# Sharing the early normalizations of an attention + PReLU-MLP kernel among three engines, with a new order of transfers and of attention pieces

## The chip, the cores and the metric

One core of one Trainium2 chip. The metric is the device time of one execution in microseconds (us). A time below is the median of a kernel's executions, which were all in the fast state except in runs 3 and 10, where the slow ones are named. The kernel before takes 353.95 us (353.81 to 354.05, four runs). Engine names in the profiles: PE is TensorE's matmuls, DVE is VectorE, ACT is ScalarE, POOL (Pool in the text) is GpSimd, SP is SyncE. PSUM is the memory into which the matmuls write, SBUF the general on-chip memory.

## The reference, cut to what matters

```python
# q, k, v: (8 batches, 8 heads, 576 positions, 64), float32
scores = q @ k.T / 8
# heads 0..3: local mask (0 <= i-j < 32); heads 4..7: strided mask (j <= i, j % 32 == i % 32)
attn = softmax(where(mask, scores, -1e9))
x = (attn @ v)  ->  (4608 tokens, 512)
h = x @ w_in                                 # 512 -> 2048
g = max(h, 0) + alpha * min(h, 0)
out = g @ w_out                              # 2048 -> 512, float32
```

The 4608 tokens are worked off in nine blocks of 512. Block 0 of layer 1 needs batch 0 of the attention, block 1 needs batch 1. Each batch has two units: the local heads and the strided heads, two pairs of heads in each.

## The kernel before

Attention is a list of small pieces that are emitted one by one between the matmuls of the two layers: T (transposes of q and k), S (scores and exponentials), P (attention times v, "PV", with the normalization), X (transpose back, into `xT`). A PV piece ends with a reciprocal of the row sums and a product, both on VectorE, read from PSUM:

```python
def pv_piece(P, a):
    ...                                      # up to 6 matmuls into pv (pool "ps", 3 PSUM buffers)
    keep(nc.vector.reciprocal(rc[0:w, 0:nb], pvv[:, :, 64]))
    keep(nc.vector.tensor_tensor(P.x16[...], pvv[:, :, 0:64], rc[...].to_broadcast(...), op=ALU.mult))
```

`keep` fixes the order: each engine executes its instructions in the order in which the program emits them. That includes the transfers: those issued by Pool (among them all that cast from float32 to float16) stand in Pool's instruction stream.

The pieces of the first two batches, and the start of the program:

```python
def alone(u0, u1):                           # u0 the strided unit, u1 the local one
    ...                                      # T(u0), S(u0) x4, T(u1), S(first pair of u1) x2,
    ...                                      # P(u0) x6, S(second pair of u1) x2, X(u0) x2, P(u1) x4, X(u1) x2

keep(nc.sync.dma_start(consts, consts_dram)) # SyncE: constants, q, k of the strided heads of batch 0
load_qk(0, True, "q")
load_qk(0, True, "k")
...                                          # Pool: rest of batch 0, w_in parts 0 to 2, strided q, k of
...                                          # batch 1, w_in part 3, v and local q, k, v of batch 1
for i in range(end0):                        # batch 0: pieces with filler matmuls between
    attn_step(end0); warm(4 if i < 2 else 1)

for c in range(4):
    load_w(c, True)                          # Pool: four w_out parts
cast_l(1, "q"); cast_l(1, "k"); ...          # Pool: casts of batch 1
load_unit(2, False); load_unit(2, True)      # Pool: ten transfers of batch 2
for m in range(16):                          # block 0 of layer 1
    lin1_piece(0, m, True)
    attn_n(0 if m < 9 else 1, end1)          # 7 pieces of batch 1 ride along
while pos["i"] < end1:
    attn_step(end1)                          # the other 19 pieces alone; then block 1
```

The softmax here doesn't subtract the row's maximum and nothing guards it: scores larger than these inputs give would overflow.

## Time and profile before

Start times from the records of the profiled run (span 352.0 us):

| | us |
|---|---|
| first k lands, cast on ScalarE begins | 7.59 |
| block 0 begins | 26.58 |
| local q, k of batch 1 transposed | 44.31, 44.76 |
| last transfer of batch 2 that Pool has to issue (stv, v of the strided heads) | 56.41 |
| block 1 begins | 57.06 |
| span | 352.0 |

Read it as two intervals: up to block 0 (26.6 us) and from block 0 to block 1 (30.5 us). After that TensorE is nearly always busy, and what is lost before it is not regained. The lines themselves stand in the prediction.

### The profile page before, as it was taken

What the parts mean: (1) busy time and instruction counts of PE and PEld (TensorE: products, weight loads), DVE (VectorE), ACT (ScalarE), POOL (GpSimd) and SP (SyncE); (2) the same over time, 40 slices, a digit from 0 to 9 for tenths busy, and PEclk for the clock granted to TensorE, in tenths of its full rate; (3) what the DMA queues carried; (4) which work ended last, traced back from release to release, by engine and by line L of the source; (5) the groups of instructions that cost most, each with busy time, mean ns of one, the idle gap of its engine ahead of it and who ended that gap; (6) DMA issues with size and microseconds to landing.
All of it is one profiled execution on the core that took longest, in us unless ns stands there. A gap on an engine that the chain in (4) does not pass through costs nothing.

```text
span 352.0 us, 6757 instructions
## 1 busy us (share of the span) xinstructions
PE 336.4 (96%) x2733; PEld 175.7 (50%) x2733; DVE 198.3 (56%) x391; ACT 176.6 (50%) x313; POOL 147.4 (42%) x164
## 2 busy tenths in 40 slices
PE   7899979999898998999999999999999999999995
PEld 2554544454444544554467665545455444444444
DVE  3487774884443875576557655765575444444400
ACT  2635852665336574656465646565645444444411
POOL 7936726259895583656365532451240000000000
PEclk9999985999999999999999999999999999999999
DMA  7999999934946862553556210000001100100021
GB/s 232 185 203 224 234 253 151 184 34 69 160 99 176 75 164 57 87 48 61 177 85 62 49 47 31 32 31 32 30 32 40 52 30 31 61 30 30 32 89 61
DMA packets 46111, 33.08 MB, mean 94 GB/s; under 512 B 27376, under 2 KB 37760, under 8 KB 46080
## 3 DMA queue, kind: packets, MB, share of 16 engines
q0 software_dynamic: 37312, 16.79, 44.6%
q1 hardware_dynamic: 8768, 15.87, 12.8%
q8 instruction: 21, 0.34, 0.4%
q14 instruction: 10, 0.08, 0.1%
HBM read 36.83 MB, written 9.44 MB: 131 GB/s over the span
## 4 chain that ended last, share of the span: by engine, by line
PE 86%; DVE 4%; POOL 4%; ACT 3%; DMA 1%; issue 1%; SPq 0%; ACTq 0%
PE hps L489 36%; PE ops L534 32%; PE sp L271 3%; PE tp L214 3%; PE pv L318 3%; DVE x L327 2%; PE xp L335 2%; POOL et L305 2%; DMA ql<-in_q_dram 1%; PE wps L556 1%; ACT kT L159 1%; PE sp L287 1%; PE ops L525 1%; ACT osb L539 1%; PE sph L287 1%
## 5 line engine op out<-in xcount | busy, mean ns | idle before, releaser
L502 DVE SCALAR_TENSOR_TENSOR gT<-neg,oma,hps 128x512 f16<-128x512 f32 x144 | 106.9, 743 | 74.7 <-ACT neg L499 72.4
L489 PE MATMUL hps<-xT,win 128*128 128x512 f16 (+1 forms) x640 | 146.7, 361 | 0.1
L534 PE MATMUL ops<-wout,gT 128*128 128x512 f16 x560 | 141.9, 379 | 1.9 <-ACT osb L539 1.6
L499 ACT ACTIVATE neg<-hps 128x512 f32<-128x512 f32 x144 | 86.2, 599 | 95.1 <-PE hps L489 93.6
L305 POOL TENSOR_TENSOR et<-et,consts 128x576 f16<-128x576 f16 (+1 forms) x48 | 61.3, 1277 | 80.5 <-ACT et L295 80.4
L489 PEld LDWEIGHTS <-win 128*128 128x128 f16 x640 | 58.4, 98 | 52.9 <-issue 3.4
L534 PEld LDWEIGHTS <-gT 128*128 128x128 f16 x560 | 49.7, 97 | 50.7 <-issue 2.5
L295 ACT ACTIVATE et<-sp 72x576 f16<-72x576 f32 (+1 forms) x58 | 37.6, 649 | 24.8 <-PE sp L271 11.7
L327 DVE TENSOR_TENSOR x<-pv,rc 72x384 f16<-72x384 f32 (+2 forms) x80 | 42.1, 527 | 2.7
L325 DVE RECIPROCAL rc<-pv 72x6 f32<-72x6 f32 (+2 forms) x80 | 14.9, 187 | 41.7 <-PE pv L318 41.4
L539 ACT COPY osb<-ops 128x512 f32<-128x512 f32 x35 | 20.6, 587 | 27.9 <-PE ops L534 27.9
L318 PEld LDWEIGHTS <-et 72*128 72x128 f16 (+1 forms) x448 | 23.2, 99 | 17.1 <-DVE x L327 1.8
L271 PEld LDWEIGHTS <-kT 64*128 64x128 f16 x448 | 10.9, 95 | 27.8 <-issue 17.7
L271 PE MATMUL sp<-qT,kT 64*128 64x72 f16 (+1 forms) x408 | 17.6, 201 | 3.5 <-ACT kT L159 3.2
L161 DVE COPY qT<-tp 128x1024 f16<-128x1024 f16 (+1 forms) x16 | 17.4, 1085 | 4.1 <-PE tp L214 4.1
L159 ACT COPY kT<-tp 128x1024 f16<-128x1024 f16 (+1 forms) x16 | 14.5, 909 | 6.7 <-PE tp L214 6.7
L556 PE MATMUL wps<-wrm 128*128 128x512 f16 x44 | 16.4, 448 | 1.2 <-DVE wrm L568 1.2
L318 PE MATMUL pv<-vs,et 72*128 72x65 f16 x256 | 15.4, 194 | 2.1 <-POOL et L305 0.8
L335 PEld LDWEIGHTS <-x 72*128 72x128 f16 (+1 forms) x224 | 12.4, 102 | 7.6 <-DVE x L327 2.4
L335 PE MATMUL xp<-consts,x 72*128 72x72 f16 (+1 forms) x224 | 14.7, 208 | 1.0 <-DVE x L327 0.8
L163 POOL COPY vs<-stv 72x1024 f16<-72x1024 f16 x14 | 14.5, 1061 | 0.0
L318 PE MATMUL pv<-vl,et 128*128 128x65 f16 x192 | 12.0, 200 | 1.2 <-DVE vl L161 1.1
(66 smaller groups left out, 189.6 us busy)
## 6 DMA issues: line engine op xcount, KB each, us to landing
out_dram<-osb SPq DMA_DIRECT2D x35, 256.0 KB, 2.0
ql<-in_q_dram SPq DMA_DIRECT2D x6, 512.0 KB, 5.2
kl<-in_k_dram SPq DMA_DIRECT2D x6, 512.0 KB, 5.9
stv<-in_v_dram POOLq DMA_DIRECT2D x8, 288.0 KB, 5.3
vl<-in_v_dram POOLq DMA_DIRECT2D x8, 288.0 KB, 8.3
win<-in_moe_w_in_dram POOLq DMA_DIRECT2D x4, 512.0 KB, 10.3
wout<-in_moe_w_out_dram POOLq DMA_DIRECT2D x4, 512.0 KB, 16.8
qs<-in_q_dram POOLq DMA_DIRECT2D x7, 256.0 KB, 4.6
```

What stands on the lines that cost most here:

```text
L271: keep(nc.tensor.matmul(sps[y][:, w * x : w * x + w], P.kT[hf, k0 : k0 + 128], P.qT[hf, w * t : w * t + w], start=(x == 0), stop=(x == len ...
L295: keep(nc.scalar.activation(ev.rearrange("r (y c) -> r y c", y=2), sp[0:r, :, 0:n], AF.Exp, scale=SCALE))
L305: keep(nc.gpsimd.tensor_tensor(ev, ev, m, op=ALU.mult))
L318: keep(nc.tensor.matmul(pv[:, 65 * x : 65 * x + 65], et[0:r, c : c + 128], v16[0:r, 2 * P.pr + hh, t, :] if P.strided else v16[:, 6 * (2 * ...
L327: keep(nc.vector.tensor_tensor(P.x16[0:w, c0 : c0 + 64 * nb].rearrange("r (c e) -> r c e", e=64), pvv[:, :, 0:64], rc[0:w, 0:nb].unsqueeze ...
L335: keep(nc.tensor.transpose(xp[:, P.w * t : P.w * t + P.w], P.x16[0 : P.w, 128 * t : 128 * t + 128], ident[0 : P.w, 0 : P.w]))
L489: keep(nc.tensor.matmul(hps[:, dst : dst + w], win16[:, kk, 128 * m : 128 * m + 128], xT[:, kk, src : src + w], start=(kk == 0 and x == 0) ...
L499: keep(nc.scalar.activation(neg, hps, AF.Relu, scale=-1.0))
L502: keep(nc.vector.scalar_tensor_tensor(gTs[n][:, m, :], neg, oma[:, m : m + 1], hps, op0=ALU.mult, op1=ALU.add))
L534: keep(nc.tensor.matmul(ops, gTs[n][:, kf, 128 * mt : 128 * mt + 128], wout16[:, kf, :], start=(kf == 0), stop=(kf == 15)))
L539: keep(nc.scalar.copy(osb, ops))
L556: keep(nc.tensor.matmul(wps, wrm[:, 0:128], wrm, start=True, stop=True))
```

## The change

The intent: VectorE's chain of reciprocals and products gates both early attention stages. Half of the products go to ScalarE (a copy from PSUM to SBUF) and Pool (the product, from SBUF), transfers are issued between Pool's products so that Pool is not blocked by a long train of them, and the strided heads of batch 1 begin inside block 0 after the fourth of its 16 tiles (index 3) instead of the tenth (index 9).

```diff
+        if P.b < NEARLY and (a == 0 or (P.strided and P.pr and a == 1)):
+            pvs = rpool.tile([128, 390], F32, tag="pvs", bufs=2, name="pvs")
+            keep(nc.scalar.copy(pvs[0:w, 0 : 65 * nb], pv[0:w, 0 : 65 * nb]))
+            pvv = pvs[0:w, 0 : 65 * nb].rearrange("r (c e) -> r c e", e=65)
+            keep(nc.gpsimd.tensor_tensor(xo, pvv[:, :, 0:64], rc[...].to_broadcast(...), op=ALU.mult))
+            return
 ...
-        feed(T(u1, "q"), -1)                       # alone(): old order cut
+        rest = [Pv(g, i) for g in A for i in range(3)]
+        if together:                               # batch 0: local transposes between the PVs
+            rest[3:3] = [T(u1, "q")]
+            rest[5:5] = [T(u1, "k")]
+        else:                                      # batch 1: PVs, transposes back, then the local unit
+            rest += [X(A[0]), X(A[1]), T(u1, "q"), T(u1, "k")]
 ...
-            hps = pspool.tile([128, 512], F32, tag="ps", name="hps3")
+            hps = popool.tile([128, 512], F32, tag="ops", name="hps3")
 ...
+    load_qk(0, True, "q")
     keep(nc.sync.dma_start(consts, consts_dram))
-    load_qk(0, True, "q")
     load_qk(0, True, "k")
 ...
+    after = {                                      # batch 0: transfers behind pieces 6, 11, 13, 23
+        6: (lambda: load_tail(1, True), lambda: load_w(2, False)),
+        11: (lambda: load_v(1, True),),
+        13: (lambda: load_w(3, False),),
+        23: (lambda: load_qk(1, False, "q"),),
+    }
 ...
+    after = {                                      # block 0: transfers and casts behind tiles 1 to 15
+        1: (lambda: load_qk(1, False, "k"),),
+        3: (lambda: load_tail(1, False), lambda: load_v(1, False)),
+        8: (lambda: load_w(0, True), lambda: cast_v(1, 0, "pool"), lambda: cast_v(1, 1, "pool"),
+            lambda: load_w(1, True)),
+        12: (lambda: load_w(2, True),),
+        14: (lambda: cast_l(1, "q"), lambda: load_w(3, True)),
+        15: (lambda: cast_l(1, "k"),),
+    }
+    for m in range(16):
+        lin1_piece(0, m, True)
+        attn_n(0 if m < 3 else 1, end1)
+        for fn in after.get(m, ()):
+            fn()
     load_unit(2, False)
     load_unit(2, True)
-    for m in range(16):
-        lin1_piece(0, m, True)
-        attn_n(0 if m < 9 else 1, end1)
     wide["on"] = True
     while pos["i"] < end1:
         attn_step(end1)
```

## The prediction

> **What bounds the kernel now.** I read the page's 40 slices first, then the chain of waits up to 96 us in order of time, Pool's timeline, the stretches around the dip of the clock, and the groups by form.
>
> ```profile
> PE   7899979999898998999999999999999999999995
> POOL 7936726259895583656365532451240000000000
> PEclk9999985999999999999999999999999999999999
> DMA  7999999934946862553556210000001100100021
> ```
>
> A slice is 8.8 us. After slice 16 TensorE is full and the edit doesn't touch it. The edit works in slices 1 to 6: attention of batch 0 (with idle-filling matmuls), layer-1 block 0, attention of batch 1, start of block 1. DMA is full from slice 1 to 7, and in slices 5 and 6 the clock dips.
>
> ```profile
> 23.54 0.55 DVE x L327
> 24.09 0.11 DVE rc L325
> 24.21 0.02 issue
> 24.23 0.55 DVE x L327
> ...
> 26.56 0.47 DVE xT L343
> 27.03 0.04 issue
> 27.07 8.58 PE hps L489 x39
> ...
> 56.70 0.42 PE xp L335 x3
> 57.12 0.53 PE hps L489
> ```
>
> This is the chain. Runs of reciprocal plus product on VectorE (0.66 us a pair) gate both attention stages. Block 0 starts at 26.6 us (fully from 27.07), block 1 at 57.06. From the last score piece inside block 0 (43.45) to 57.06 only attention runs. Whatever moves the start of block 1 moves the end one for one, since what follows is unchanged.
>
> ```profile
> 50.00:51.00 1.00, 0.81 (x17) 0.50 (x14) 0.96 (x4) 0.00 (x0) 0.00 (x0) 0.85 1.52 302
> 51.00:52.00 1.00, 1.00 (x9) 0.34 (x8) 0.93 (x4) 0.45 (x1) 0.34 (x1) 0.50 1.76 270
> ...
> 60.00:61.00 1.00, 1.00 (x4) 0.30 (x3) 0.58 (x1) 0.09 (x1) 1.00 (x2) 0.53 1.20 205
> 61.00:62.00 1.00, 1.00 (x6) 0.48 (x5) 0.46 (x1) 0.61 (x2) 1.00 (x2) 1.00 1.09 255
> ```
>
> The granted clock (third number from the end) is 0.50 from 50.9 to 60.9 us, so block 1 runs 3.9 us at half speed and loses about 1.9.
>
> ```profile
> 47.23 0.72 POOL L111 DMA_DIRECT2D qs<-in_q_dram  x1 [4.17 <-DMA wout<-in_moe_w_out_dram]
> 49.11 0.71 POOL L111 DMA_DIRECT2D ks<-in_k_dram  x1 [1.16 <-DMA wout<-in_moe_w_out_dram]
> 51.66 0.57 POOL L130 DMA_DIRECT2D tl<-in_q_dram  x1 [1.85 <-DMA wout<-in_moe_w_out_dram]
> 53.66 0.55 POOL L130 DMA_DIRECT2D tl<-in_k_dram  x1 [1.42 <-DMA ql<-in_q_dram]
> 56.41 0.76 POOL L144 DMA_DIRECT2D stv<-in_v_dram  x1 [2.21 <-DMA kl<-in_k_dram]
> ```
>
> This is the view I weigh most. Counted in Pool's own order, every transfer waits for the one eight before it to land: the 32nd (qs of batch 2) for the 24th (second w_out part), the 36th (stv of batch 2) for the 28th (kl of batch 2), which lands at 56.1. The same holds at 16.57, 18.26, 21.68 and 24.32. In the kernel before nobody needs Pool between 38 and 57 us, so these waits are free.
>
> **What the Trainium skill says.** "GPSIMD Engine Reference", section 1: Pool has no PSUM access; hence the ScalarE copy ahead of each Pool product. Its section 3.1: about 2.6 cycles per element for a two-input operation at 1.2 GHz. For 576 columns that is 1,248 ns; the trace's mask products take 1,277, so it agrees. "DMA: Bandwidth & Descriptors", "Anatomy of one DMA": a wait for a semaphore is served by the issuing sequencer, not by the DMA engines. The lines above agree: Pool itself stands still. "TensorE: Matmul & The Clock Gate", Part 1: the clock halves after a sparse window of some 3.4 us and comes back after a busy one. The dip of 10.0 us (three windows) agrees.
>
> **The change part by part.**
>
> ```profile
> L327 DVE TENSOR_TENSOR x<-pv,rc 96x384 f16<-96x384 f32 x32 | 17.7, 553 | 1.1
> ...
> L305 POOL TENSOR_TENSOR et<-et,consts 128x576 f16<-128x576 f16 x24 | 30.7, 1278 | 48.1 <-ACT et L295 48.1
> ...
> L539 ACT COPY osb<-ops 128x512 f32<-128x512 f32 x35 | 20.6, 587 | 27.9 <-PE ops L534 27.9
> ```
>
> (a) *Normalizations.* In each of batches 0 and 1, 5 of the 10 products (384 columns) leave VectorE: 5 x 0.55 = 2.8 us off. ScalarE gets 5 copies of 390 columns; from 587 ns at 512 columns and 266 at 128 (0.84 ns a column) that is 0.49 each, 2.4 us. Pool gets 5 products, 384 x 2.6 / 1.2 GHz = 0.83, with dispatch about 0.95 (estimate), 4.8 us. One offloaded piece goes from 0.74 us (reciprocal, product) to 0.49 + 0.95 = 1.44: longer by itself, only the throughput improves.
>
> (b) *Order in batch 0.* The PVs of the strided pairs come ahead of the local transposes. From 13.5 us (end of the strided scores, as now): PV1 to PV3 fill the three PSUM buffers; the first is free when ScalarE, done with its exponentials at 14.1, has copied it, 14.65. So the q transpose is at 14.75 (13.56 before), its VectorE half 15.5 to 16.2 and ScalarE half to 16.8 (they go one after the other in the trace), the copy of PV4 17.3, kT 17.85, VectorE's half of kT 18.6, which frees the buffer for the sixth PV. Local scores: 19.0 and 19.85, then 21.1 and 21.9, against 16.1, 16.9, 20.5 and 21.3. The last exponential ends at 23.2, the copy of x^T 23.85, the local PV copies 24.35 and 24.85, Pool's two products 25.3 and 26.3, last x^T 27.1. Block 0 starts about 26.9, +0.3: VectorE is relieved, ScalarE becomes the limit. q ahead of the constants on the queue saves 0.3 us that the k load (landing 7.55) swallows.
>
> (c) *More attention inside block 0.* 13 pieces instead of 7 ride in it. Matmul time: 16 x 0.862 = 13.8, transposes 1.2, four score pieces 0.59 each = 2.4, six PVs 1.2, one transpose back 0.26: 18.8 us, from 26.9 to 45.7. The layer-1 tile in place of a "ps" buffer is neutral. The stretch left alone loses its VectorE run of 48.3 to 52.2: some 4 us of possible gain, the main prize.
>
> (d) *Pool's order there.* Products of block 0 follow ScalarE's copies: the fourth strided PV at about 43.3 to 44.2, third w_out part to 45.0 (0.74), the next product to 45.9, cast of ql to 47.0 (1.05), fourth w_out part to 47.7, cast of kl to 48.7. So the local k transpose is at 48.8 (44.8 before) and local scores 50 to 52; exponentials end at 53.2. Then ten transfers of batch 2 stand ahead of the last two products: 2 x 0.73 + 2 x 0.63 + 1.2 + 2 x 0.71 + 2 x 0.55 + 0.75 = 7.2 us, to 55.9 without a wait. The last of them waits for the landing of kl of batch 2. That queue carried the same bytes before and landed it at 56.1. Now the third w_out part is issued at 44.3 instead of 31.6, leaving the queue dry near 42 to 44, while the q and k of batch 3 on the other queue, released by the casts, move from 34.8 to 47 and compete there (before, they stretched a nominal 9 us of Pool's queue to 13.6). Without competition kl lands near 54, with it 56 to 57.5; I take 56.3. Products to 59.2, first x^T ready about 59.0. Block 1 starts at about 59, +2.0. The 4 us of (c) are consumed by Pool's queue.
>
> (e) *Clock.* The sparse stretch is no shorter: again a dip, again 3.4 to 6.8 us of block 1 in it, loss 1.7 to 3.4 against 1.9 now; I add nothing in the middle, up to +1.5 outside.
>
> Sum: (b) +0.3 is contained in (d), +2.0; with a small discount, as an edit with this much placing was probably tuned: +1.5.
>
> **Rivals.** *Gain kept:* if Pool's last two products were not held, they would follow the copies at about 53.7; the local transposes back would end near 56, or 53 if the casts of ql and kl also came early. That makes 350 to 353 us. For: VectorE really was in the chain. Against: the product order is fixed, and 7.2 us of issues alone stand in front. *First stage faster:* if ScalarE and VectorE overlap better than in (b), block 0 starts at 25 and all of Pool's work moves 1.5 to 2 us up: 352 to 354. *Clock falls in batch 0:* PV pieces of small matmuls between 14.8 and 19 us, with one filler each, are sparser than now (I count about 45% of a window against 55%; the stretch before the dip at 50.9 had about 40%). Block 0 would then start later and half-speed: +3 to +4, 357 to 360. *Weights late:* w_in parts 3 and 4 are issued among Pool's products, yet by the trace's pace of 2.7 to 3.1 us a part they land near 27 and 32, needed near 35 and 42: hidden.
>
> **Range and chances.** Middle 355.4. Two independent doubts, about 2 us each (landing of kl, start of block 0), and a clock term that mostly adds: 351.5 to 359.5. Faster by 2% means under 346.8: block 1 would have to start at 50, which ten issues forbid: 0.03. Slower means over 360.9: needs the clock in the first stage and the late landing together: 0.08. Within: 0.89.
>
> **What would show it.** Right: Pool products of batch 1's local pairs starting after 55 us, with the wait of the stv transfer just before; block 0 starting between 26 and 28; local scores of batch 0 near 19; about 0.95 us a Pool product; VectorE idle before the last x^T. Wrong: kl of batch 2 landing before 53, or block 1 starting by 55 with ScalarE or TensorE as the last wait; a clock under 1.0 before 40 us.

## The result, and the profile after

The changed kernel takes 364.46 us (362.66 to 365.67, four runs), against 353.95: 1.0293 times as long, 95% interval 1.0239 to 1.0348. A ratio here is the mean time of one kernel's fast runs over that of the other's of the same rounds, so not quite the ratio of the medians. Executions over 1.5% slower than the fastest of the same kernel are left out of the means. The predicted range, 351.5 to 359.5, was missed.

Three rows of the page first (40 slices, counted from 0, now of 9.1 us each; a digit is the busy share in tenths, in PEclk the clock that TensorE was granted, in tenths of full speed):

```profile
PE   6798975599989898999999999999999999999996
...
PEclk9899996599999999999999999999999999999999
DMA  7999959991394677157335630000000010010012
```

Three things are new: TensorE is at 0.6 and 0.7 in the first two slices, where it was 0.7 and 0.8, and the clock dips in the second; TensorE is half idle in slices 6 and 7, with a dip of the clock (before, the dip lay in slices 5 and 6); and DMA, full from slice 1 to 7 before, has a hole in slice 5 (about 46 to 55 us). Now the chain that ended last, in order of time (start, length, what):

```profile
2.15 8.30 DMA kl<-in_k_dram
10.45 0.02 issue
10.47 1.05 ACT ks L159
...
31.08 3.40 PE hps L498 x15
...
50.39 0.98 POOL ql L163
51.37 0.75 POOL wout L554
52.12 1.05 POOL kl L163
53.17 0.64 POOL ql L111
53.81 12.05 DMA kl<-in_k_dram
65.86 0.28 issue
66.14 0.75 POOL stv L144
66.90 1.62 POOL x L332 x2
68.52 0.05 issue
68.57 0.68 PE xp L342 x6
```

There are two DMA waits of k in it, and neither was on the chain before. The first is the very first k: it lands at 10.45 us instead of 7.57, so block 0 begins at 30.59 (26.58 before). ScalarE's record of its cast in the kernel before:

```profile
7.59 1.05 ACT L159 CAST ks<-kl 128x1024 f16<-128x1024 f32 x1 [5.57 <-DMA kl<-in_k_dram]
```

The second is batch 2's k: Pool issues it at 53.81, it lands 12.05 us later, and only then may Pool issue stv, behind which stand the last two normalization products of batch 1. Pool's own timeline shows the wait:

```profile
56.98 0.72 POOL L111 DMA_DIRECT2D qs<-in_q_dram  x1
57.69 0.71 POOL L111 DMA_DIRECT2D ks<-in_k_dram  x1
60.28 0.58 POOL L130 DMA_DIRECT2D tl<-in_q_dram  x1 [1.88 <-DMA wout<-in_moe_w_out_dram]
62.44 0.55 POOL L130 DMA_DIRECT2D tl<-in_k_dram  x1 [1.58 <-DMA ql<-in_q_dram]
66.14 0.75 POOL L144 DMA_DIRECT2D stv<-in_v_dram  x1 [3.15 <-DMA kl<-in_k_dram]
66.90 1.61 POOL L332 TENSOR_TENSOR x<-pvs,rc 96x384 f16<-96x384 f32 x2
```

ScalarE had copied the inputs of these two products by 61.0 us; Pool starts on them at 66.90. TensorE waits 7.48 us for them, and block 1 begins at 69.03 (57.06 before):

```profile
67.80 1.44 PE L342 MATMUL xp<-consts,x 96*128 96x96 f16 x12 [7.48 <-POOL x L332]
```

| profiled run | block 0 begins | from block 0 to block 1 | block 1 begins | span |
|---|---|---|---|---|
| before | 26.58 | 30.48 | 57.06 | 352.0 |
| after | 30.59 | 38.44 | 69.03 | 363.9 |
| difference | +4.0 | +8.0 | +12.0 | +11.9 |

So the loss is all there by the start of block 1, a third of it ahead of block 0. The profiled run is one of the two slower of the four (365.65 us).

The moved operations themselves cost what was estimated, or a little less:

```profile
L332 POOL TENSOR_TENSOR x<-pvs,rc 72x384 f16<-72x384 f32 (+1 forms) x10 | 8.5, 859 | 17.6 <-ACT pvs L330 17.6
...
L330 ACT COPY pvs<-pv 72x390 f32<-72x390 f32 (+1 forms) x10 | 4.8, 479 | 2.6 <-DVE rc L327 2.4
```

0.86 us a product on Pool (0.95 was estimated), 0.48 a copy on ScalarE (0.49).

### The profile page after: what moved, and what is told of

It is laid out like the page before. It is cut to its first block, busy times and chain, and to the rows that moved or that the text cites. A ratio compares the mean times of both kernels' runs of the same rounds, so it can differ in the third digit from the quotient of the medians.

```text
span 363.9 us, 6771 instructions
## 1 busy us (share of the span) xinstructions
PE 337.6 (93%) x2733; PEld 175.9 (48%) x2733; DVE 192.8 (53%) x381; ACT 180.7 (50%) x323; POOL 155.2 (43%) x174
## 4 chain that ended last, share of the span: by engine, by line
PE 80%; POOL 6%; DMA 6%; ACT 3%; DVE 3%; issue 1%; SPq 0%; ACTq 0%; DVEq 0%; POOLq 0%
PE hps L498 34%; PE ops L543 31%; DMA kl<-in_k_dram 6%; PE sp L271 3%; PE tp L214 3%; PE pv L318 3%; PE xp L342 2%; POOL et L305 2%; PE wps L565 1%; POOL x L332 1%; PE ops L534 1%; DVE x L336 1%; PE sp L287 1%; DVE gT L511 1%; ACT kT L159 1%
## 5 line engine op out<-in xcount | busy, mean ns | idle before, releaser
L336 DVE TENSOR_TENSOR x<-pv,rc 96x384 f16<-96x384 f32 (+2 forms) x70 | 36.6, 523 | 2.4
L548 ACT COPY osb<-ops 128x512 f32<-128x512 f32 x35 | 20.5, 585 | 27.9 <-PE ops L543 27.9
L332 POOL TENSOR_TENSOR x<-pvs,rc 72x384 f16<-72x384 f32 (+1 forms) x10 | 8.5, 859 | 17.6 <-ACT pvs L330 17.6
```

Source lines behind the costliest of these rows:

```text
L336: keep(nc.vector.tensor_tensor(xo, pvv[:, :, 0:64], rc[0:w, 0:nb].unsqueeze(2).to_broadcast([w, nb, 64]), op=ALU.mult))
L548: keep(nc.scalar.copy(osb, ops))
```

## The experiments

Two theories came out of the traces. **Q**: the constants, issued between the first q and k, made k late. **H**: the last two products are held in Pool's order behind transfers of batch 2. The first four runs shared one chip; the kernel before, run beside them, had a median of 353.91 us (seven runs).

**1. Constants first.** The changed kernel with the old order on SyncE's queue:

```diff
-    load_qk(0, True, "q")
     keep(nc.sync.dma_start(consts, consts_dram))
+    load_qk(0, True, "q")
     load_qk(0, True, "k")
```

> The changed kernel with the constants again ahead of q on SyncE's queue, nothing else. Theory Q: the constants between q and k made the first k land at 10.45 us instead of 7.57; undone, k lands near 7.6, the clock stays at 1.0 before 40 us, block 0 starts near 27.5 instead of 31.1 and the total falls by 3 to 3.5 us to about 361. Rival: the first w_in part, issued at 7.8 instead of 10.0 us, crowds k out: then k still lands after 9.5 and the total stays at 364.

Measured: 361.04 us (360.51 to 363.5), ratio to before 1.0215 (1.0177 to 1.0253). The first k lands at 7.56, block 0 begins at 26.18, 4.4 us earlier than in the changed kernel, though the total falls only by 3.4, because batch 2's k takes still longer here (below). The first w_in part was issued at 7.79 us, as in the changed kernel (7.78). Since k had landed just before, this run alone doesn't dismiss that rival; run 5 does, where k is late though the first w_in part is issued only at 9.98, after it has landed.

**2. Local pairs of batch 1 on VectorE.** Two of the ten products go back:

```diff
-        if P.b < NEARLY and (a == 0 or ...):
+        if P.b < NEARLY and (P.strided or P.b == 0) and (a == 0 or ...):
```

> The changed kernel, but the local pairs of batch 1 are normalized on VectorE as before (8 products stay offloaded instead of 10). Theory H: these two products stood on Pool behind the stv transfer of batch 2, which waits for kl to land (65.9 us); without them block 1 starts near 62 instead of 69.5 and the total falls by 7 to 8 us to about 357. Rival: the transfers themselves are late (the queue ran dry from 44 to 50 us) and batch 2's data hold block 1 or its attention pieces: gain under 3 us, a DMA wait in the chain elsewhere.

Measured: 357.59 us (355.92 to 358.6), ratio 1.0088 (1.0054 to 1.0123): 6.9 us less than the changed kernel. Block 1 begins at 62.45. Pool still issues stv at 66.92 and waits 3.81 us for it, but now nobody waits for Pool. H holds; batch 2's data being late did not matter.

**3. Batch 2's transfers behind the last pieces of batch 1.** All ten products stay offloaded:

```diff
-    load_unit(2, False)
-    load_unit(2, True)
     wide["on"] = True
     while pos["i"] < end1:
         attn_step(end1)
+    load_unit(2, False)
+    load_unit(2, True)
```

> The changed kernel with the ten transfers of batch 2 issued after the last attention pieces of batch 1 in Pool's order. Theory H: products no longer held, block 1 starts near 62, total 356 to 358 as in the run with VectorE. Rival of timing: batch 2's q and k land some 8 us later (near 72), so that the transposes at the end of block 1 wait and half of the gain is given back: 359 to 361.

Measured: 357.13 and 361.14 us in two fast runs, 364.33 and 366.36 in two slow. The trace of the 361.14 run shows one source of the spread: the first k lands at 10.34, much as in the changed kernel, TensorE runs dry, and here the clock was at 0.50 from 11 to 24 us (in the changed kernel from 12 to 16), so block 0 began only at 34.05. From block 0 to block 1 it took 30.7 us (64.77 less 34.05) instead of 38.4. That part agrees with H, and the start had to be taken out of the comparison, which run 6 does.

**4. Constants first and local pairs on VectorE**, runs 1 and 2 together.

> Both: constants first and the local pairs of batch 1 on VectorE. If Q and H are independent the gains add: 364 less 3.3 less 7.5, about 353.5, level with the kernel before. If the start is swallowed by a later wait (casts or transfers in Pool's order), it stays at 356 to 357.

Measured: 354.06 us (352.17 to 354.23), ratio 0.9992 (0.9963 to 1.0021). The two losses add up (3.4 and 6.9 of 10.4 us), and with both undone nothing is left of the slowdown. But nothing of the intended gain is left either: block 0 begins at 26.25, block 1 at 58.06. In TensorE's timeline one sees what delays it then:

```profile
46.10 0.34 PE L342 MATMUL xp<-consts,x 72*128 72x72 f16 x5 [0.61 <-POOL x L332]
47.08 0.62 PE L214 MATMUL tp<-consts,ql 128*128 128x128 f16 x8 [0.64 <-POOL ql L163]
48.86 1.04 PE L214 MATMUL tp<-consts,kl 128*128 128x128 f16 x8 [1.16 <-POOL kl L163]
```

Every one of these waits is for Pool: for a product, then for the casts of q and k that stand behind the products and w_out parts in its order. The second transpose takes 1.04 us instead of 0.62, the clock being at half.

The next four runs shared another chip (before: 353.90 us, seven runs).

**5. The constants' place alone, in the kernel before.** The only edit to that kernel:

```diff
-    keep(nc.sync.dma_start(consts, consts_dram))
     load_qk(0, True, "q")
+    keep(nc.sync.dma_start(consts, consts_dram))
     load_qk(0, True, "k")
```

> The kernel before with only one edit: the constants issued between the first q and k on SyncE's queue. Theory Q: k lands near 10.4 us instead of 7.57, TensorE runs dry from 8.5 to 11 us, block 0 starts 3 to 4 us later, total about 357. Rival (the first w_in part issued early did it): k lands by 8, total stays at 354.

Measured: 358.58 us (356.85 to 359.27), ratio 1.0140 (1.0111 to 1.0168): one moved line costs 4.7 us. The chain of waits of this run, its start:

```profile
1.52 0.58 SPq L570
2.10 0.05 issue
2.15 7.62 DMA kl<-in_k_dram
9.76 0.02 issue
9.78 1.05 ACT ks L159
```

k is issued 0.2 us later than in the kernel before (2.15 against 1.95) and lands 2.2 us later. Everything behind shifts: block 0 at 28.77, block 1 at 59.43, the stretch between them 30.7 us, nearly unchanged. This trace is of the fastest of the four runs (356.85 us, 2.9 above the kernel before); what the other three lost beyond that stands in no trace.

**6. Constants first and batch 2's transfers later** (edits of runs 1 and 3).

> The changed kernel with the constants first and batch 2's ten transfers behind the last attention pieces: the run with the transfers later, without the uneven start that spread its times from 357 to 366. Theory H: it gives the same as constants first plus VectorE, 353 to 355, since only the place of the two products in Pool's order matters. Rival: batch 2's data, issued some 6 us later, are waited for near 75 us: 356 or more.

Measured: 355.18 us (354.32 to 356.51), ratio 1.0040 (1.0010 to 1.0071), 5.9 us less than run 1. Block 0 begins at 26.89 (the first k landed at 8.25 here), and it takes 30.8 us from block 0 to block 1. So it is the place of the two products in Pool's order that carries most of the 7 us, not the engine that computes them. The one us more than in run 4 may be the rival's (stv is issued at 63.74 instead of 60.30) or come from the later k; it is too small to be assigned.

**7. Casts and w_out parts earlier in Pool's order**, on top of run 4:

```diff
-        8: (w_out part 0, cast of v, cast of v, w_out part 1),
-        12: (w_out part 2,),
-        14: (cast of q, w_out part 3),
-        15: (cast of k,),
+        8: (w_out part 0, cast of v, cast of v, w_out part 1, cast of q, cast of k, w_out parts 2, 3),
```

> Constants first, local pairs of batch 1 on VectorE, and the casts of batch 1's q and k and the last two w_out parts issued with the others after block 8 (Pool has nothing to do there from 34 to 40 us). Theory P: Pool's order is also what holds the local transposes of batch 1 at 47.1 and 48.9 us; with the casts done by 37 the transposes run by 46.5, block 1 starts near 54.5 instead of 58.1 and the total is 350 to 351. Rival: VectorE's or ScalarE's work for the layer-1 tiles or the halved clock is the next limit: 352.5 to 354.

Measured: 350.46 us (350.44 to 352.06), ratio 0.9915 (0.9887 to 0.9943), as theory P (Pool's order also holds the local transposes) said. The two transposes start at 45.57 and 46.44, at full clock, and block 1 begins at 54.60:

```profile
45.57 0.61 PE L214 MATMUL tp<-consts,ql 128*128 128x128 f16 x8
46.44 0.61 PE L214 MATMUL tp<-consts,kl 128*128 128x128 f16 x8 [0.26 <-ACT xT L346]
```

This beats both kernels, by 0.85% over the kernel before. It is inside the 2% that count as "same" here, but clear of noise.

**8. The early heads alone, in the kernel before.** Strided heads of batch 1 from the fourth tile and the new order of pieces for batch 1 (with the layer-1 tile moved out of pool "ps"), nothing else:

```diff
-        attn_n(0 if m < 9 else 1, end1)
+        attn_n(0 if m < 3 else 1, end1)
-            hps = pspool.tile(..., tag="ps", name="hps3")
+            hps = popool.tile(..., tag="ops", name="hps3")
 # alone(3, 2): P(u0) x6, X(u0) x2 ahead of T(u1), as in the change
```

> The kernel before with only the third part of the edit: strided heads of batch 1 from the fourth layer-1 tile in the new order of pieces, all normalizations on VectorE, all transfers where they were. If interleaving alone carries the gain that the prediction gave it (some 4 us), block 1 starts near 53.5 and the total is 350. Rival: without relief VectorE falls behind between the layer-1 tiles and the PV pieces (1.4 us of work a step against 1.06 of TensorE), and the total is 352 to 354.

Measured: 353.6 us (352.38 to 353.99), ratio 0.9987 (0.9959 to 1.0014). Block 1 begins at 56.70, against 57.06. The rival was right: VectorE is busy without a gap from 39.5 to 48.0 us, and TensorE waits for it at the end of block 0:

```profile
44.92 1.02 PE L497 MATMUL hps<-xT,win 128*128 128x512 f16 x4 [0.20 <-DVE gT L510]
45.78 0.62 PE L335 MATMUL xp<-consts,x 72*128 72x72 f16 x14
46.82 0.24 PE L335 MATMUL xp<-consts,x 72*128 72x72 f16 x2 [0.42 <-DVE x L327]
47.16 0.61 PE L214 MATMUL tp<-consts,ql 128*128 128x128 f16 x8
```

The transposes begin 1.6 us later than in run 7 (47.16 against 45.57). Interleaving without relief for VectorE moves the queue, not the end.

The last four (same chip as the four above; before: 353.86 us, eight runs).

**9. The new orders without the offload**: run 7 with every product on VectorE.

> The run with casts after block 8 (350.5 us), but every normalization on VectorE: the new orders of pieces and transfers without the offload. If the offload is what pays (VectorE's queue is the limit once PV pieces ride inside block 0, as the run with the early heads alone suggests), block 1 starts near 57 and the total is 353 to 354. If the orders of pieces and transfers pay, it stays at 350 to 351.

Measured: 352.94 us, spread from 350.14 to 354.13, ratio 0.9947 (0.9900 to 0.9995). The interval overlaps that of run 7, so the worth of the offload is not settled: in the profiled run, the slowest of the four, block 1 begins at 56.94 (54.60 in run 7). The four times go with the mean granted clock: 350.14 us at 0.998, 352.55 at 0.989, 353.33 at 0.985, 354.13 at 0.981. In the best run the clock hardly dipped, and there VectorE alone did as well as three engines. What the offload may buy is a dip less often; four runs don't show it, nor which of the two, dip or wait, brings the other.

**10. All ten products offloaded, with the three mends of order**: constants first, casts and w_out parts after tile 8, batch 2's transfers behind the last pieces.

> All ten products offloaded as the change has it, with the three queue mends: constants first, casts and w_out parts after block 8, batch 2's transfers behind the last pieces of batch 1. Theory: the offload of the last two products is harmless once nothing stands in front of them, so 350 to 352. Rival: the later transfers of batch 2 (issued near 55 us) or the longer copy-and-product path cost 2 us or more: 352.5 to 355.

Measured: the three fast runs took 350.61, 350.9 and 350.92 us, ratio 0.9912 (0.9882 to 0.9942). So the change's idea, with its orders mended, is as good as run 7. But two of the five executions took 358.89 and 359.94 us, among them the profiled one. Five executions are too few to call this version the less steady one, and what slowed these two is not tested.

**11. Batch 3's local q and k issued by Pool**, on top of run 1, so that they come behind batch 2's in one queue instead of beside them in another:

```diff
-        eng = nc.sync if (b > 2 and not strided) or ... else nc.gpsimd
+        eng = nc.sync if (b > 3 and not strided) or ... else nc.gpsimd
```

> The changed kernel with constants first (361.0 us), and batch 3's local q and k issued by Pool in its order instead of SyncE, so that they no longer share the engines with batch 2's q and k at 47 to 62 us. Theory C: the 13 us landing of batch 2's k (7 assumed in the prediction) is that sharing; without it k lands near 57 instead of 62.4, block 1 starts near 60.5 instead of 65.7 and the total is about 356. Rival: Pool's own queue is slow by itself (small rows of tails and v): k still lands after 61 and the total stays at 360 to 361.

Measured: 356.3 us (356.17 to 358.16), ratio 1.0081 (1.0050 to 1.0112), 4.7 us less than run 1 (on another chip, where the kernel before took the same to 0.1 us). Batch 3's q and k are now issued at 61.13 and 61.91 instead of beside batch 2's. Their issues, and the chain, in run 1 and then in run 11:

```profile
46.98 0.61 SPq L111 DMA_DIRECT2D ql<-in_q_dram  x1
48.78 0.60 SPq L111 DMA_DIRECT2D kl<-in_k_dram  x1
...
49.39 12.97 DMA kl<-in_k_dram
62.65 0.75 POOL stv L144
63.41 1.62 POOL x L332 x2
```

```profile
61.13 0.79 POOL L111 DMA_DIRECT2D ql<-in_q_dram  x1
61.91 0.72 POOL L111 DMA_DIRECT2D kl<-in_k_dram  x1
...
49.44 7.11 DMA kl<-in_k_dram
56.84 0.50 POOL stv L144
```

Batch 2's k, issued at the same time, lands after 7.11 instead of 12.97 us, and block 1 begins at 59.73 instead of 65.54. "DMA: Bandwidth & Descriptors", section "Issuing engines are not separate DMA queues", of the Trainium skill says that transfers issued by different engines run on the same 16 DMA engines and interleave. The traces agree: with batch 3's q and k in flight at the same time, batch 2's k lands 5.9 us later. The run changes the queue of these two transfers and so their time; it doesn't tell the two apart.

**12. The constants behind the first k**, in the kernel before: order q, k, constants.

> The kernel before with the constants issued behind the first k. If what delays k is the constants in front of it in the same queue, k lands by 7.6 as before; the constants then land late, after 7 us, and since VectorE handles them ahead of the cast of q the start is late all the same: total 355 to 357. Rival: any start with q first delays k (whatever stands between): k lands after 9 us.

Measured: 356.66 us (356.07 to 357.03), ratio 1.0077 (1.0056 to 1.0099). Now k lands at 7.00, so it is the constants between q and k, not q at the head, that delay k; but the constants land at 7.45, and VectorE, which handles them first, can cast q only at 7.79 (6.04 before). The clock is at 0.50 from 9 to 12 us, and block 0 begins at 29.45. Constants first is the best of the three orders. How 122 KB in the middle of the queue cost the next transfer 2 us (k lands 7.6 us after its issue in run 5), when at its head they cost next to nothing (5.6 us with them there, in the kernel before, and 5.5 with them behind k, in run 12), is left open.

## Why the prediction was wrong

Its main mechanism was right: what freeing VectorE and interleaving win is consumed by Pool's order, and the last two products stand behind stv, which waits for batch 2's k. Its middle was +1.5 us, the result +10.5. Two terms were wrong, and both are queues of transfers. The prediction had named the pair, a clock that falls in the first stage together with a late landing, as what a slower kernel would need, and given it 0.08.

- **(b), "q ahead of the constants on the queue saves 0.3 us that the k load (landing 7.55) swallows".** This is the first failed step: it looked at q alone and took the landing of k as given. It measured 10.45 (runs 1, 4, 5 and 12 show it by the constants' place). TensorE then idles, the clock falls for about 3 us (0.50 from 13 to 15 us), and block 0 begins at 30.59 instead of the 26.9 predicted. With the constants first, in run 4, it begins at 26.25, and the local scores of batch 0 at 18.4, 19.2, 20.5 and 21.3, against 19.0, 19.85, 21.1 and 21.9 in the prediction: the rest of (b) was sound and, by about 0.6 us, pessimistic.
- **(d), "Without competition kl lands near 54, with it 56 to 57.5; I take 56.3".** This is the second failed step: the mechanism was right and the size was off. Without the late start (run 1) k lands at 62.4, that is 12.97 us after its issue at 49.39; the prediction's step allowed 7. Run 11 takes the competition away: 7.11 us, landing at 56.55. So both parts were too small: the landing without competition by 2.5 us (54 against 56.55), and the competition from batch 3's q and k, counted as 2 to 3.5 us, which measures 5.9. That run 11 meets the predicted start of block 1 (59.73 against about 59) is luck: the prediction had the competition in it, run 11 has none. The prediction had seen the move from 34.8 to 47 us and the dry queue (DMA's hole), but had no landing measured under such a load: the one that it started from, 56.1 in the kernel before, came 17.0 us after its issue. Its figures in brackets there (9 us stretched to 13.6) can't be retraced from the lines that it shows.
- **(d), Pool's order before that.** Local k transposed at 48.8: measured 48.86 in run 4, but after a block 0 that began 0.65 us earlier than predicted, so the agreement to the tenth is partly luck. Products waiting at Pool, stv's wait just before them: as written.
- **(a), the operations**: right within 0.1 us each. "GPSIMD Engine Reference", section 3.1, has 2.6 cycles an element for two inputs: the products of 384 columns took mostly 0.82 us, which is 2.56 cycles at the page's 1.2 GHz, so the dispatch that the prediction added on top (0.12 us) was not there.
- **(c), "some 4 us of possible gain"**: 26.28 to 54.60 in run 7 is 28.3 us against 30.5 before, so 2.2 us, about half of it, once Pool's order lets it out; the total gains 3.4.
- **(e), the clock**: a dip that reaches 3.4 to 6.8 us into block 1 was expected, and the one from about 63.3 to 73.6 us reaches some 4.6 us into it. That it is a second one, after a dip from 53 to 60 us, was not expected, nor was the one near 13 us, which is one of the prediction's own signs of being wrong (a clock under 1.0 before 40 us). In the trace the dips follow stretches in which TensorE is little busy (it waits 7.5 us ahead of block 1); that the idling causes them is argued, not tested. The "about 40%" that the prediction counted ahead of the dip at 50.9 is not the profile's busy share: from 47.5 to 50.9 us that is 68% (2.30 of 3.40 us).
- **Rivals**: "weights late" did not happen: TensorE has no wait for a w_in part in block 0. "Clock falls in batch 0" did, but from the late k, not from sparse pieces; in run 4, with the same pieces and k on time, the clock stays at 1.0 up to 48 us.

The prediction's +1.5 against +10.5 is thus: some 3.4 us for the constants (run 1), 4.7 for the competition (run 11 against run 1), and 0.9 for the middle being taken low (run 11 is at 356.3, the prediction at 355.4). These are differences of successive runs, so that they sum to 9.1 (364.46 less 355.4) is no further evidence; the experiments show the first two.

## What to carry to other kernels

An engine that both computes and issues transfers serves its instructions in order: before a product is moved to it, list what stands ahead of the product, and for each transfer what its issue waits for; two products behind ten transfers cost 7 us here (run 2), and moving the ten transfers behind the two products gave 5.9 of them back (run 6). A transfer's landing time is no property of the transfer: when a change moves an issue, find what else will be in flight at the new time, on every queue, and read the landing from a time with a like load. The cheapest edit of a list, such as one line of order at the start, deserves its own run.

## What the Trainium skill lacked or had wrong

- "DMA: Bandwidth & Descriptors" gives about 2.0 us plus bytes over 436 GB/s for one transfer. That is one transfer by itself; no page gives a landing time for one that has others in flight around it. Here a transfer of 512 KB took 7.11 us behind one queue's backlog and 12.97 us beside a second queue (runs 11 and 1).
- The same page says that a wait is served by the issuing sequencer, but no page counts how many transfers may be in flight. In this program, in Pool's own order, a transfer that has to wait waits for the landing of the one eight before it (3.15 us for stv); whether that is the program's semaphores or the chip, no run here tells.
- "SBUF — State Buffer", section "SBUF: two separate sides", says that GpSimd and some VectorE operations lock a shared port pair for a whole instruction, and that the other engine blocks. It doesn't say how many instructions in a row one can be made to wait. That the port is the cause of what follows is not tested. A copy that VectorE does in 0.54 us took 1.49 beside Pool in the kernel before, and in one slow execution of run 10 it spanned 8.78 us, ending 0.4 us after the last of eight Pool instructions (the longest 1.29 us) that ran one after another. This is one record of a slow run.

```profile
73.04 8.78 DVE L161 COPY vl<-vl 32x1495 f16<-32x1495 f16 x1
```

- "TensorE: Matmul & The Clock Gate", Part 1, lets the clock fall after an "idle window"; it gives no busy share at which one counts as idle. Here TensorE was busy for 22% of the 3.4 us ahead of one fall (12.1 us in the changed kernel), for 29% ahead of another (53.2 us) and for 68% ahead of a third (50.9 us in the kernel before), while a busy share of 61% from 44.1 to 47.5 us in the kernel before led to none. Its "<1% of a typical kernel span" is said of the ramp at the start of a kernel, and no page says how far one kernel's time spreads when the clock falls again later. Here run 9 went from 350.14 to 354.13 us with the granted clock at 0.998 and 0.981, more than the whole gain that was sought.
